# Running rows on ACT's queue and as one-row products, with new half steps in the first two blocks

## The chip, the cores and the metric

One Trainium2 chip, one core. The metric is the device time of one execution in microseconds (us). In the profile PE is TensorE's matmul stream and PEld its weight loads, DVE is VectorE, ACT is ScalarE, POOL is GpSimd, SP is SyncE, whose queue issues the kernel's transfers; "ACTq" or "SPq" is such an engine's queue.

## The reference

A token block of 2048 x 448 passes two stages, each behind a layer norm whose scale, shift and gate come from a condition vector `c` (six groups of `c @ w_mod`). The first stage is an S4 convolution: each channel d has a kernel K[d, l], the real part of a sum over 256 complex modes, and the stage adds the gated convolution of the normalized tokens with K, plus a skip term. The second is a SwiGLU network:

```python
h = silu(y @ w_gate) * (y @ w_up)      # 448 -> 1792
out = x + gate * (h @ w_down)          # 1792 -> 448
```

## The kernel before

**Tiles and blocks.** The tokens are 16 tiles of 128 rows, in blocks of 2, 2, 3, 3, 3 and 3 tiles (`BLOCKS`). With the given data the kernel K is so close to a straight line in l that the convolution is a pair of running sums along the tokens: v0 and v1 are the normalized tile times two gain rows (`gm0`, `gm1`), and a product with a triangle of ones (`tri`) gives their sums within the tile. The sums up to the tile's start are one row each, `run0` and `run1` (1 x 448 f32). A flag computed on the device picks this path; a general convolution stands in the other branch and is not run.

**The network.** `ffn` goes over 14 slices f of 128 of the 1792 hidden channels. `gate_up(f)` is 22 products (L665), w and y each split into a coarse and a fine f32r part; then come silu on ACT (L671), the mult on DVE (L676), the cast `phi` on ACT (L679) and its rest `plo` on DVE (L680). `down(f - 1)` (L691) is three products a tile that add into one PSUM bank a tile. So TensorE's order is gate_up(f), down(f-1), gate_up(f+1), down(f), and on. In block 0 the weights are not in SBUF yet: each slice loads w(f+5) (L85, L86: gate and up, four transfers) and the w_down rows d(f+3) (L92) on SP's queue, and ACT and DVE split them: `split_d` of slice f (L96 ACT, L97 DVE) at the head of gate_up(f), `split_w` of f + 2 (L103, L104 ACT; L106, L108 DVE) around its silu.

**The stages of the next tiles.** The first stage of the next block's tiles is hung into the running block, at half steps: 2f is behind gate_up(f), 2f + 1 behind down(f - 1). The table `TIMES` holds a row for block 0, one for block 1, and one for all later ones: the half steps of the first norm's statistics for each tile, of its root, then for each tile those of its stages with the second norm's statistics as the last, of the second root, and of the normalized tiles (`make_xn`, L185). Each engine runs its instructions in program order, so a half step too early makes the engine wait, and all that is behind it too. The stages are s0 (`make_h`, L170 and L172), s1 (v0 and v1, L784), `rows` (the running rows are added to row 0 of v0 and v1, L789 and L790), s2 (`rows`, then the coarse and fine part of v0, L797 ACT and L798), s3 (h times the skip gain), s4 (three products with `tri`, L809 to L811) and s5. Block 0 leaves s2 out and has s4f, with the product of v0 in f32 (L820, L821).

s5 makes the running rows of the next tile: a copy on ACT (L830), `run0` on DVE (L831), both in partitions 96 to 127, and a transfer of partition 127 to partition 0 (L832, `run[0:1] <- run[127:128]`, both rows, 3.5 KB). Two more DVE instructions (L833, L834) finish the tile. The next tile's `rows` read what the transfer brought. There are 13 such transfers.

**Ahead of block 0.** Tiles 0 and 1 are computed in a prelude. Its end is `transposes(TILES[0])`, which turns the normalized tiles and splits them into `hhi` and `hlo` (L192 PE, L193 and L195 ACT, L197 and L198 DVE; the third of its four banks is the PSUM buffer `cv`), and then six products of 33 x 448 (L442) into `cv`, which give the running rows behind tile 1, copied out on ACT (L445, L446). Buffers of `bank()` come from a pool of four PSUM banks, `cv` is one by itself.

Of the kernel before, what the change touches and what calls it, by code (L numbers as in the profile page):

```python
# [8 lines left out]
F32 = mybir.dt.float32  # L9
# [7 lines left out]
L, D, N, F = 2048, 448, 256, 1792  # L17
# [6 lines left out]
TILES = [list(range(sum(BLOCKS[:b]), sum(BLOCKS[:b + 1]))) for b in range(len(BLOCKS))]  # L24
# [2 lines left out]


TIMES = (
# [3 lines left out]
)  # L33
EPS = 1e-5
# [5 lines left out]
def f32(ap):  # L40
    return ap.bitcast(F32)
# [3 lines left out]
def tile_kernel(ctx, tc, x, a_re, a_im, b_re, b_im, c_re, c_im, log_dt, dskip,  # L45
                wg, wu, wd, c, w_mod, dft, idft, out):
    nc = tc.nc
    sy, ve, sc, po, pe = nc.sync, nc.vector, nc.scalar, nc.gpsimd, nc.tensor
# [4 lines left out]
    psd = ctx.enter_context(tc.tile_pool(name="psd", bufs=1, space=PS))  # L53
    dram = ctx.enter_context(tc.tile_pool(name="dram", bufs=1, space=bass.MemoryType.DRAM))

    def bank():
        t = psg.tile([128, 512], F32, name="bank")
        return t
# [40 lines left out]
    def split_w(j, part=None):  # L99
        hi, lo, st = wgu[j][:, :, 0:3, :], wgu[j][:, :, 3:6, :], wgu[j][:, :, 6, :]  # L100
        w = raw[j]
        if not part:
            sc.copy(hi, w[:, :, 0:3, :])  # L103
            sc.copy(st, w[:, :, 3, :])  # L104
        if part is None or part == 1:
            ve.tensor_tensor(lo, w[:, :, 0:3, :], f32(hi), op=OP.subtract)  # L106
        if part is None or part == 2:
            ve.tensor_tensor(st[64:128], w[64:128, :, 3, :], f32(st[64:128]), op=OP.subtract)  # L108

    ident = const.tile([128, 128], F32)  # L110
    tri = const.tile([128, 128], F32R)
    tok = const.tile([128, 1], F32)

    run = const.tile([128, 2, D], F32)
    run0, run1 = run[:, 0, :], run[:, 1, :]
# [71 lines left out]
    def transposes(ts):  # L187
        n = len(ts) * 128
        for k in range(4):
            ps = psd.tile([128, 512], F32, name="cv") if k == 2 else bank()  # L190
            for j, i in enumerate(ts):
                pe.transpose(ps[:, j * 128:(j + 1) * 128], xn[i][:, k * 128:(k + 1) * 128], ident)  # L192
            sc.activation(hhi[:, k, 0:n], ps[:, 0:n], AF.Identity, scale=cb1c[:, k:k + 1], bias=sbc[:, k:k + 1])  # L193
            if k % 2:
                sc.activation(ps[:, 0:n], ps[:, 0:n], AF.Identity, scale=cb1c[:, k:k + 1], bias=sbc[:, k:k + 1])  # L195
            else:
                ve.tensor_scalar(ps[:, 0:n], ps[:, 0:n], cb1c[:, k:k + 1], sbc[:, k:k + 1], op0=OP.mult, op1=OP.add)  # L197
            ve.tensor_tensor(hlo[:, k, 0:n], ps[:, 0:n], f32(hhi[:, k, 0:n]), op=OP.subtract)  # L198
# [61 lines left out]
    with tc.tile_pool(name="pre", bufs=1) as pre, tc.tile_pool(name="wm", bufs=6) as wm:  # L260
# [86 lines left out]
        s0 = pre.tile([P, 4], F32)  # L347
# [33 lines left out]
        for k in range(3):  # L381
# [13 lines left out]
        v0, v1, vh, vl, hd = ([pre.tile([128, D], t, name=f"{n}_{q}") for q in range(2)] for n, t in  # L395
                              (("v0", F32), ("v1", F32R), ("vh", F32R), ("vl", F32R), ("hd", F32)))
# [38 lines left out]
        ve.tensor_scalar(flag, zm, SMALL * SMALL, None, op0=OP.is_le)  # L435
        for z in (1, 2):
            split_w(0, z)
        transposes(TILES[0])
        o = psd.tile([128, 512], F32, name="cv")[:, 0:D]
        mm = [(left[:, 0], v) for v in vh + vl] + [(left[:, 1 + q], v1[q]) for q in range(2)]  # L440
        for k, (u, v) in enumerate(mm):
            pe.matmul(o[0:33], u, v, start=k == 0, stop=k == len(mm) - 1)  # L442
        split_w(1)
        sc.copy(xs[1], os[1])
        sc.copy(run0[0:1], o[0:1])  # L445
# [322 lines left out]
    def small_path(pools):  # L768
        work = pools.work
        vs = {}  # L770

        def s0(i):
            h = work.tile([128, D], F32, name="h", bufs=2)
            make_h(h, i)
            vs[i] = h

        def s1(i, on_v=False):
            h = vs[i]  # L780
            v0 = work.tile([128, D], F32, name="v0", bufs=2)
            v1 = work.tile([128, D], F32R, name="v1", bufs=2)
            for v, g in ((v0, gm0), (v1, gm1)):
                (ve if on_v else po).tensor_tensor(v, h, g, op=OP.mult)  # L784
            vs[i] = h, v0, v1

        def rows(i, on_v=False):
            h, v0, v1 = vs[i]
            ve.tensor_tensor(v0[0:1], v0[0:1], run0[0:1], op=OP.add)  # L789
            (ve if on_v else po).tensor_tensor(v1[0:1], f32(v1[0:1]), run1[0:1], op=OP.add)  # L790

        def s2(i, on_v=False):
            rows(i, on_v)
            h, v0, v1 = vs[i]
            vh = work.tile([128, D], F32R, name="vh")
            vl = work.tile([128, D], F32R, name="vl")
            sc.copy(vh, v0)  # L797
            ve.tensor_tensor(vl, v0, f32(vh), op=OP.subtract)  # L798
            vs[i] = h, vh, vl, v1

        def s3(i, on_v=False):
            h = vs[i][0]
            (ve if on_v else po).tensor_tensor(h, h, gd, op=OP.mult)

        def s4(i):
            h, vh, vl, v1 = vs[i]
            o = psd.tile([128, 512], F32, name="cv")[:, 0:D]
            s = bank()[:, 0:D]
            pe.matmul(o, tri, vh, start=True, stop=False)  # L809
            pe.matmul(s, tri, v1, start=True, stop=True)  # L810
            pe.matmul(o, tri, vl, start=False, stop=True)  # L811
            ve.tensor_tensor(xs[i], h, xs[i], op=OP.add)
            vs[i] = o, s


        def s4f(i):
            h, v0, v1 = vs[i]
            o = psd.tile([128, 512], F32, name="cv")[:, 0:D]
            s = bank()[:, 0:D]
            pe.matmul(s, tri, v1, start=True, stop=True)  # L820
            pe.matmul(o, f32(tri), v0, start=True, stop=True)  # L821
            s3(i, True)
            ve.tensor_tensor(xs[i], h, xs[i], op=OP.add)
            vs[i] = o, s

        def s5(i):
            o, s = vs.pop(i)
            if i + 1 < NT:
                e = slice(96, 128)
                sc.copy(run1[e], s[e])  # L830
                ve.scalar_tensor_tensor(run0[e], run1[e], 128.0, o[e], op0=OP.mult, op1=OP.add)  # L831
                sy.dma_start(run[0:1], run[127:128])  # L832
            ve.tensor_tensor(xs[i], xs[i], o, op=OP.add)  # L833
            ve.scalar_tensor_tensor(xs[i], s, tok, xs[i], op0=OP.mult, op1=OP.add)  # L834

        v = lambda g: lambda i: g(i, True)
        return lambda b: ((s0, v(s1), v(rows), s4f, s5), (s0, v(s1), v(s2), v(s3), s4, s5),
                          (s0, s1, s2, s3, s4, s5))[min(b, 2)]

    def general_path(pools, y):  # L840
# [81 lines left out]
```

## Time and profile before

| what | us |
| --- | --- |
| median of 3 runs | 517.26 |
| lowest and highest run | 516.23, 518.02 |
| the profiled execution, its time | 516.48 |
| its span | 514.7 |
| TensorE busy | 485.2 |
| VectorE busy | 278.3 |
| ScalarE busy | 163.9 |
| block 0's first gate_up starts | 51.65 |
| block 1's first gate_up starts | 116.76 |
| block 2's first gate_up starts | 179.58 |

The mean granted clock of TensorE over the span was 0.973 of full speed. A row of a timeline reads: start, length, engine, line, operation, what it writes <- what it reads, and in brackets how long the engine stood still just before and what ended that. A row of waits reads: who waited, for whom, the total, how often, and the longest.

### The profile page before, as it was taken

The page shows a single profiled execution, that of the slowest core. Times are in us where ns is not written, and L with a number is a line of the kernel's source. Part 1 is how long each engine was busy: PE and PEld are TensorE (multiplying, and loading weights), DVE is VectorE, ACT ScalarE, POOL GpSimd, SP SyncE. Part 2 cuts the span into 40 slices and gives each one's busy share as a digit, 9 for nine tenths or more (in the row PEclk, how much of TensorE's full clock was granted, in tenths as well). Part 3 has the DMA queues.
Part 4 walks back from the last instruction along what each step waited for, and adds up shares of the span by engine and source line. Part 5 has one row for each costly group of instructions (what it writes and reads, how often), then busy time and mean ns, then how long its engine had stood idle before and what let it go on. Part 6 is the DMA issues. An engine that isn't in the chain of part 4 may idle for free.

```text
span 514.7 us, 7042 instructions
## 1 busy us (share of the span) xinstructions
PE 485.2 (94%) x2747; PEld 453.5 (88%) x2747; DVE 278.3 (54%) x516; ACT 163.9 (32%) x346; POOL 87.3 (17%) x103
## 2 busy tenths in 40 slices
PE   7867998899998999999999999999999999999994
PEld 4443988799997899999999999999999999999993
DVE  1897699956785563464374555455345346112213
ACT  4248554562222621221441122162122143111110
POOL 1468000000000102341100532000234110000000
PEclk8888999899998999999999999999999999999998
DMA  7995355512000020000020000003000001000001
GB/s 204 263 228 172 112 152 162 155 41 91 1 0 2 2 90 1 0 2 0 2 95 14 1 2 2 0 1 107 1 1 2 0 3 55 0 1 1 1 0 60
DMA packets 26002, 26.05 MB, mean 51 GB/s; under 512 B 2248, under 2 KB 25288, under 8 KB 25960
## 3 DMA queue, kind: packets, MB, share of 16 engines
q1 hardware_dynamic: 25960, 25.52, 17.5%
q8 instruction: 23, 0.38, 0.3%
q14 instruction: 19, 0.16, 0.1%
HBM read 21.80 MB, written 3.67 MB: 49 GB/s over the span
## 4 chain that ended last, share of the span: by engine, by line
PE 79%; DVE 6%; SPq 6%; DMA 4%; issue 3%; ACT 1%; POOL 0%; DVEq 0%; ACTq 0%; POOLq 0%
PE bank L665 51%; PE dn L691 24%; SPq L85 3%; SPq L86 2%; DMA br<-in_A_B_re_dram 2%; DMA raw<-in_B_w_up_dram 1%; PE bank L192 1%; DMA run<-run 1%; DVE gu L106 1%; DVE gu L108 1%; SPq L275 1%; DMA rawd<-in_B_w_down_dram 1%; DVE wdl L97 1%; DVE bank L676 1%; PE cv L809 1%
## 5 line engine op out<-in xcount | busy, mean ns | idle before, releaser
L665 PE MATMUL bank<-hhi,gu 128*128 128x384 f32 (+1 forms) x1169 | 211.3, 320 | 0.0
L665 PEld LDWEIGHTS bank<-hhi,gu 128*128 128x128 f32 x1169 | 191.6, 190 | 3.4 <-issue 0.7
L665 PE MATMUL bank<-hlo,gu 128*128 128x384 f32 (+1 forms) x668 | 131.9, 318 | 0.0
L676 DVE TENSOR_TENSOR bank<-raw,bank 128x384 f32<-128x384 f32 (+1 forms) x70 | 37.5, 535 | 154.3 <-PE bank L665 137.7
L665 PEld LDWEIGHTS bank<-hlo,gu 128*128 128x128 f32 x668 | 110.3, 190 | 0.3 <-DVE hlo L198 0.3
L679 ACT CAST phi<-bank 128x384 fp32r<-128x384 f32 (+1 forms) x84 | 37.3, 444 | 145.1 <-DVE bank L676 145.1
L671 ACT ACTIVATE raw<-bank 128x384 f32<-128x384 f32 (+1 forms) x70 | 32.8, 469 | 128.7 <-PE bank L665 128.5
L680 DVE TENSOR_TENSOR plo<-bank,phi 128x384 fp32r<-128x384 f32 (+1 forms) x84 | 43.0, 512 | 38.0 <-ACT phi L679 38.0
L691 PE MATMUL dn<-wdh,phi 128*128 128x448 f32 x224 | 61.3, 373 | 0.5 <-ACT phi L679 0.5
L691 PE MATMUL dn<-wdl,phi 128*128 128x448 f32 x224 | 60.0, 368 | 0.0
L691 PE MATMUL dn<-wdh,plo 128*128 128x448 f32 x224 | 59.9, 367 | 0.0
L691 PEld LDWEIGHTS dn<-wdl,phi 128*128 128x128 f32 x224 | 42.3, 189 | 4.0
L691 PEld LDWEIGHTS dn<-wdh,plo 128*128 128x128 f32 x224 | 41.9, 188 | 4.1
L691 PEld LDWEIGHTS dn<-wdh,phi 128*128 128x128 f32 x224 | 39.9, 190 | 2.6 <-ACT phi L679 1.1
L151 POOL TENSOR_SCALAR rsb<-mvb 128x3 f32<-128x3 f32 (+1 forms) x6 | 1.7, 282 | 124.5 <-DVE mvb L135 124.5
L784 POOL TENSOR_TENSOR v<-h,gm 128x448 f32<-128x448 f32 x9 | 11.1, 1237 | 64.5 <-DVE h L172 55.0
L151 POOL TENSOR_SCALAR rsa<-mva 128x3 f32<-128x3 f32 (+1 forms) x6 | 1.6, 268 | 108.1 <-DVE mva L135 108.1
L209 PE MATMUL bank<-wmt,cs 112*128 112x448 f32 (+1 forms) x32 | 16.1, 662 | 2.3 <-DMA wmt<-in_w_mod_dram 2.3
L209 PEld LDWEIGHTS bank<-wmt,cs 112*128 112x128 f32 (+1 forms) x32 | 6.4, 209 | 10.6 <-issue 9.7
L106 DVE TENSOR_TENSOR gu<-raw,gu 128x768 fp32r<-128x768 f32 x14 | 14.6, 1041 | 0.4 <-ACT gu L103 0.3
L790 POOL TENSOR_TENSOR v<-v,run 1x448 fp32r<-1x448 f32 x9 | 11.4, 1270 | 17.3 <-DMA run<-run 17.1
L797 ACT CAST vh<-v 128x448 fp32r<-128x448 f32 x12 | 6.8, 567 | 20.7 <-DVE v L789 20.7
(194 smaller groups left out, 447.6 us busy)
## 6 DMA issues: line engine op xcount, KB each, us to landing
wmt<-in_w_mod_dram SPq DMA_DIRECT2D x6, 784.0 KB
rawd<-in_B_w_down_dram SPq DMA_DIRECT2D x14, 224.0 KB
x<-in_A_u_dram SPq DMA_DIRECT2D x12, 224.0 KB
raw<-in_B_w_gate_dram SPq DMA_DIRECT2D x14, 192.0 KB
raw<-in_B_w_up_dram SPq DMA_DIRECT2D x14, 192.0 KB
out_dram<-x SPq DMA_DIRECT2D x11, 224.0 KB
raw<-in_B_w_gate_dram SPq DMA_DIRECT2D x14, 64.0 KB
raw<-in_B_w_up_dram SPq DMA_DIRECT2D x14, 64.0 KB
```

Of the source, the lines that this page charges most:

```text
L85: sy.dma_start(raw[j][:, s, 0:3, :], w[0:384, cs].rearrange("(k p) f -> p k f", p=128))
L86: sy.dma_start(raw[j][:, s, 3, :], bass.AP(tensor=w.tensor, offset=w.offset + 384 * F + j * 128, ap=[[0, 2], [F, 64], [1, 128]]))
L106: ve.tensor_tensor(lo, w[:, :, 0:3, :], f32(hi), op=OP.subtract)
L209: pe.matmul(ps[0:rows, 0:D], cs[:, k:k + 1].to_broadcast([P, rows]), w[k], start=k == 0, stop=k == 3)
L665: pe.matmul(ps[s][:, 0:n], w[:, s, a], (hlo if lo else hhi)[:, k, 0:n], start=not lo and a == 0, stop=lo and k == 3)
L671: sc.activation(p[:, 0:n], ps[0][:, 0:n], AF.Silu)
L676: ve.tensor_tensor(ps[1][:, 0:n], p[:, 0:n], ps[1][:, 0:n], op=OP.mult)
L679: sc.copy(hi[:, 0:n], ps[1][:, 0:n])
L680: ve.tensor_tensor(lo[:, 0:n], ps[1][:, 0:n], f32(hi[:, 0:n]), op=OP.subtract)
L691: pe.matmul(dn[q][:, 0:D], u[:, cs], v, start=f == 0 and z == 0, stop=f == NF - 1 and z == 2)
L784: (ve if on_v else po).tensor_tensor(v, h, g, op=OP.mult)
L790: (ve if on_v else po).tensor_tensor(v1[0:1], f32(v1[0:1]), run1[0:1], op=OP.add)
```

## The change

Four things are edited.

1. The rows of `TIMES` for block 0 and block 1 have other numbers; the row for the later blocks stays. In block 0 the stages `rows` are gone from the lists.
2. In the prelude the six products come ahead of the transposes and write into a `bank()` instead of `cv`.
3. In block 0 `rows` is left out. Instead s4f adds two f32 products of one row each (`tri[0:1]` with `run1` and with `run0`, new lines L823 and L824) into the same PSUM sums.
4. The transfer of the running rows is issued by ACT (new line L835) and no longer by SP.

Behind s4f the new file has three lines more (L831 becomes L834, L833 becomes L836).

```diff
 TIMES = (
-    ((1, 3), 3, ((4, 6, 7, 9, 10, 12), (8, 11, 14, 16, 17, 18)), 19, (20, 21)),
+    ((1, 1), 3, ((4, 7, 10, 12, 14), (3, 8, 19, 19, 21)), 22, (25, 23)),
...
-        transposes(TILES[0])
-        o = psd.tile([128, 512], F32, name="cv")[:, 0:D]
+        o = bank()[:, 0:D]
...
             pe.matmul(o[0:33], u, v, start=k == 0, stop=k == len(mm) - 1)
+        transposes(TILES[0])
...
-            pe.matmul(s, tri, v1, start=True, stop=True)
-            pe.matmul(o, f32(tri), v0, start=True, stop=True)
+            pe.matmul(s, tri, v1, start=True, stop=False)
+            pe.matmul(o, f32(tri), v0, start=True, stop=False)
+            pe.matmul(s, f32(tri[0:1, :]), run1[0:1], start=False, stop=True)
+            pe.matmul(o, f32(tri[0:1, :]), run0[0:1], start=False, stop=True)
...
-                sy.dma_start(run[0:1], run[127:128])
+                sc.dma_start(run[0:1], run[127:128])
...
-        return lambda b: ((s0, v(s1), v(rows), s4f, s5), (s0, v(s1), v(s2), v(s3), s4, s5),
+        return lambda b: ((s0, v(s1), s4f, s5), (s0, v(s1), v(s2), v(s3), s4, s5),
```

For block 1's third tile `TIMES` goes from (13, 16, 20, 19, 21, 22, 22) to (13, 17, 17, 18, 20, 21, 21), and the root and the normalized tiles from 23 and (24, 24, 25) to 25 and (25, 25, 25).

TensorE in block 0, around the first tile's s4f. Before, in the fifth slice (`wdl_533` and `wdh_532` are parts of w_down, `gu_527` the next gate and up weights):

```order
L691 MATMUL dn_489<-wdl_533,phi 128x448
L691 MATMUL dn_488<-wdh_532,plo 128x448
L691 MATMUL dn_489<-wdh_532,plo 128x448
L820 MATMUL bank<-v_700,tri 128x448
L821 MATMUL cv<-v_699,tri 128x448
L665 MATMUL bank<-hhi,gu_527 128x256 x7
L665 MATMUL bank<-hlo,gu_527 128x256 x4
```

and now:

```order
L691 MATMUL dn_489<-wdh_532,plo 128x448
L665 MATMUL bank<-hhi,gu_527 128x256 x7
L665 MATMUL bank<-hlo,gu_527 128x256 x4
L665 MATMUL bank<-hhi,gu_527 128x256 x7
L665 MATMUL bank<-hlo,gu_527 128x256 x4
L821 MATMUL bank<-v_709,tri 128x448
L822 MATMUL cv<-v_708,tri 128x448
L823 MATMUL bank<-run,tri 128x448
L824 MATMUL cv<-run,tri 128x448
L691 MATMUL dn_488<-wdh_584,phi 128x448
```

The tri products moved from ahead of the next gate_up to behind it, and the two one-row products stand behind them; the second tile's moved from behind a gate_up at half step 16 to behind a down at 19.

ACT in block 0, around the first run row (what an instruction waits for stands in the brackets; a name with DMAHW is a transfer's semaphore). Before:

```order
L679 CAST phi<-bank 128x256 [waits DVE_49]
L830 COPY run<-bank 32x448
L96 CAST wdh_696<-rawd_76 128x448 [waits DMAHW5_49]
L671 ACTIVATE p<-bank 128x256 [waits PE_49,Activation_49]
L103 CAST gu_691<-raw_75 128x2x384 [waits DMAHW3_49,DMAHW1_49]
```

and now:

```order
L679 CAST phi<-bank 128x256 [waits DVE_49]
L833 COPY run<-bank 32x448
L835 DMA run<-run 1x16x56 [waits DMAHW3_49,DVE_49]
L96 CAST wdh_754<-rawd_77 128x448 [waits DMAHW2_49]
L671 ACTIVATE p<-bank 128x256 [waits PE_49]
```

The issue stands between the copy and the next split of w_down, a slice later than the copy did, and waits for DVE and for a semaphore that the weight loads use too.

DVE in block 1, behind the second tile's s5 (rawd_77 is the second tile, x_68 the third, v_1639 and v_1657 its v0). Before:

```order
L831 SCALAR_TENSOR_TENSOR run<-run,cv 32x448
L833 TENSOR_TENSOR rawd_77<-rawd_77,cv 128x448
L834 SCALAR_TENSOR_TENSOR rawd_77<-bank,tok,rawd_77 128x448
L134 BN_STATS stb<-rawd_77 128x6
L135 BN_AGGR mvb<-stb 128x2
L803 TENSOR_TENSOR h<-h,gd 128x448
L676 TENSOR_TENSOR bank<-raw_74,bank 128x256
L680 TENSOR_TENSOR plo<-bank,phi 128x256
L789 TENSOR_TENSOR v_1639<-v_1639,run 1x448
L790 TENSOR_TENSOR v_1640<-v_1640,run 1x448
L798 TENSOR_TENSOR vl<-v_1639,vh 128x448
L812 TENSOR_TENSOR x_68<-h,x_68 128x448
```

and now:

```order
L834 SCALAR_TENSOR_TENSOR run<-run,cv 32x448
L836 TENSOR_TENSOR rawd_77<-rawd_77,cv 128x448
L837 SCALAR_TENSOR_TENSOR rawd_77<-bank,tok,rawd_77 128x448
L784 TENSOR_TENSOR v_1657<-h,gm_86 128x448
L784 TENSOR_TENSOR v_1658<-h,g_85 128x448
L789 TENSOR_TENSOR v_1657<-v_1657,run 1x448
L790 TENSOR_TENSOR v_1658<-v_1658,run 1x448
L798 TENSOR_TENSOR vl<-v_1657,vh 128x448
L676 TENSOR_TENSOR bank<-raw_74,bank 128x256
L680 TENSOR_TENSOR plo<-bank,phi 128x256
L134 BN_STATS stb<-rawd_77 128x6
L135 BN_AGGR mvb<-stb 128x2
```

The third tile's v0, v1 and running rows moved ahead of a slice's mult and `plo`, directly behind the run row's own end, and the second tile's statistics moved behind them.

2 rows, old and new, of the table TIMES are left out of this document.

## The prediction

> **What bounds the kernel now.** I read the page's head first, then TensorE's waits, then tables of clock and traffic for single stretches, then the timelines around the waits.
>
> ```profile
> span 514.7 us, 7042 instructions
> ...
> PE 485.2 (94%) x2747; PEld 453.5 (88%) x2747; DVE 278.3 (54%) x516; ACT 163.9 (32%) x346; POOL 87.3 (17%) x103
> ```
>
> TensorE is busy 94% of the span, so outside the opening the kernel is a TensorE program, and a change that is no TensorE saving can win only what TensorE loses by standing still or by a slow clock. Its waits (total, times, longest):
>
> ```profile
> PE bank L820 <- DVE v L790: 3.9, 2, 3.0
> ...
> PE cv L442 <- DVE hlo L198: 2.9, 1, 2.9
> ...
> PE cv L809 <- ACT vh L797: 2.2, 1, 2.2
> ...
> PE bank L192 <- ACT raw L185: 1.0, 2, 0.7
> ```
>
> L820 is block 0, L442 the end of the prelude, L809 and L192 block 1. In the next table the columns are busy time (PE, PEld, DVE, ACT, POOL), then TensorE's granted clock, DMA share and GB/s.
>
> ```profile
> 57.00:60.00 3.00, 3.00 (x23) 2.91 (x22) 2.31 (x4) 3.00 (x7) 0.00 (x0) 1.00 0.11 32
> 62.00:88.00 26.00, 24.54 (x169) 22.59 (x168) 25.31 (x50) 14.08 (x32) 1.17 (x2) 1.00 0.55 159
> 92.50:94.50 2.00, 2.00 (x5) 1.08 (x4) 1.94 (x5) 0.90 (x2) 0.00 (x0) 0.50 0.62 193
> 118.00:159.00 41.00, 41.00 (x299) 39.98 (x298) 30.87 (x63) 10.04 (x25) 1.11 (x2) 1.00 0.09 29
> 163.00:166.00 3.00, 3.00 (x17) 3.00 (x15) 0.00 (x0) 0.39 (x1) 0.00 (x0) 0.50 0.02 5
> ```
>
> Three things: 41 us of block 1 run without a gap at full clock; right behind the waits of block 0 and block 1 the clock is 0.50; and the weight stream of block 0 moves 159 GB/s, but only 32 between 57 and 60 us.
>
> Now the two places. Block 0 (start, length, engine; in brackets the idle time before and what ended it), then the chain of waits for the same place:
>
> ```profile
> 72.58 0.47 PE L820 MATMUL bank<-v,tri 128*128 128x448 f32 x1 [0.96 <-DVE v L790]
> ...
> 73.29 0.63 PE L665 MATMUL bank<-hhi,gu 128*128 128x256 f32 x1
> ...
> 91.72 0.74 PE L820 MATMUL bank<-v,tri 128*128 128x448 f32 x1 [2.98 <-DVE v L790]
> ...
> 95.41 0.76 PE L665 MATMUL bank<-hhi,gu 128*128 128x256 f32 x5
> ...
> 116.76 1.00 PE L665 MATMUL bank<-hhi,gu 128*128 128x256 f32 x7
> ```
> ```profile
> 86.62 3.87 DMA run<-run
> ...
> 122.19 1.22 PE dn L691 x6
> ...
> 123.41 2.63 PE bank L665 x22
> ```
> ```profile
> 80.24 0.63 DVE L831 SCALAR_TENSOR_TENSOR run<-run,cv 32x448 f32<-32x448 f32 x1
> ```
>
> The row was ready at 80.87 (80.24 + 0.63), its transfer was issued only at 86.62, behind weight loads on SP's queue, and took 3.87. TensorE paid 0.96 + 2.98 in waits. The pair of products and one `down` took 3.69 (91.72 to 95.41) where 0.71 (72.58 to 73.29) + 1.22 = 1.93 is the full-clock price: 1.76 lost to the clock. Sum 5.7.
>
> Block 1:
>
> ```profile
> 150.85 0.36 PE L809 MATMUL cv<-vh,tri 128*128 128x448 f32 x1
> ...
> 154.10 0.57 PE L691 MATMUL dn<-wdh,phi 128*128 128x448 f32 x2
> ...
> 161.55 0.47 PE L809 MATMUL cv<-vh,tri 128*128 128x448 f32 x1 [2.21 <-ACT vh L797]
> ...
> 166.65 0.57 PE L691 MATMUL dn<-wdh,phi 128*128 128x448 f32 x2
> ```
>
> The same work, tri products and a gate_up (2.63 of it the gate_up, by the chain's row), took 5.10 at 161.55 and 3.25 at 150.85: 1.85 lost to the clock, 2.21 to the wait, and 1.0 to the late last normalization (the L192 row). Sum 5.1.
>
> **The change, part by part.**
>
> *Block 1, new steps.* The third tile's `s2` comes directly behind the second's `s5` (both at half step 17, where they were at 17 and 20), with its tri products at 20 now, so that three half steps lie between where one lay. The danger is that the run row now travels between these two. Rows from quiet stretches (DVE, POOL), two from the chain of waits in block 0, and the split's second half:
>
> ```profile
> 230.36 0.63 DVE L831 SCALAR_TENSOR_TENSOR run<-run,cv 32x448 f32<-32x448 f32 x1
> ...
> 232.82 1.14 POOL L790 TENSOR_TENSOR v<-v,run 1x448 fp32r<-1x448 f32 x1 [5.64 <-DMA run<-run]
> ```
> ```profile
> 82.15 1.15 DVE v L784 x2
> ...
> 91.06 0.62 DVE v L790
> ```
> ```profile
> 161.53 0.63 DVE L798 TENSOR_TENSOR vl<-v,vh 128x448 fp32r<-128x448 f32 x1
> ```
>
> From the end of L831 (230.99) to the reader's start: 1.83 us. Behind L831 VectorE now has what it had in block 0 behind the L831 of 80.24: L833, L834 and two L784, from 80.87 to 83.30 (82.15 + 1.15), 2.43. The row lands 0.6 before VectorE asks for it. Followed on: call T the end of gate_up(8). down(7) and the tri products end at T+1.84 (1.22 + 0.62), the copy on ACT (0.53, quoted below) and the run row (0.63) at T+3.0, VectorE reaches the row additions at T+5.4, two of 0.62 and the split's 0.63 end at T+7.3, and the mult and the cast of slice 9 (0.4 each, the cast's row is below) at T+8.1. TensorE needs the cast at T+8.94 (1.84, then 2.63 + 1.22 + 2.63 + 0.62). Margin 0.8, so the wait of 2.21 goes and its slow stretch with it. A row flight of 3.87, as beside the weights, would be 1.4 past VectorE's arrival, less the margin: 0.6 of wait. The last statistics come some slices earlier, and the normalization follows slice 12's cast directly: the 1.0 goes. What is late next: nothing that I can price. Gain 5.1, bounds 3 (a wait of 2 comes back) and 5.5.
>
> *Run row on ACT's queue.* Thirteen issues leave SP, where one took 0.65 and another waited 5.75 for its turn (80.87 to 86.62), and come to ACT ahead of the next silu or, in block 0, of the next split of w_down.
>
> ```profile
> 79.81 1.98 SPq L92 DMA_DIRECT2D rawd<-in_B_w_down_dram  x1
> ...
> 86.62 0.65 SPq L832 DMA_DIRECT2D run<-run  x1
> ```
> ```profile
> 217.88 0.53 ACT L830 COPY run<-bank 32x448 f32<-32x448 f32 x1
> ...
> 220.54 0.49 ACT L671 ACTIVATE raw<-bank 128x384 f32<-128x384 f32 x1 [2.13 <-PE bank L665]
> ```
>
> Ahead of the second row's silu, in block 2, ACT idles 2.13 behind a run-row copy; it must now wait 0.7 for VectorE's part of the run row (0.63) and issue for 0.65: 1.35, hidden. In block 1, with shorter slices, some tenths may stick out. Behind the issue only the silu waits, and TensorE needs that slice's cast a whole gate_up later (2.63 in block 1). ACT's price of an issue isn't in the trace (ACT issues nothing before): between nothing and the 1.98 that the longest SP issue of a weight load could be; I take 0.65, the same transfer's row. At 1.98 ACT is held 2.7, 0.55 over the idle time, and a gate_up covers that: also nothing. Without that cover the 8 issues of blocks 2 to 4 would cost 8 x 0.55 = 4.4. SP loses its waits for the row, and its loads move up by 0.65 in each of two slices, which is inside the stream's bounds below.
>
> *Block 0: one-row products.* VectorE loses four 1-row additions (0.6 each). TensorE gains four f32 products. An f32 product of this width is what stands between 72.58 and 73.29 beside one f32r product: 0.71 for both, so about 0.4 to 0.5; 4 x 0.4 = 1.6 us added to TensorE, certain unless TensorE stands there anyway. The first tile needs only the prelude's row. The second tile's run row is made behind half step 12 and read at 19, three and a half slices: about 13 us against 0.65 + 3.87. So the waits at L820 and their slow stretch go (5.7), less 1.6: 4.1 on TensorE.
>
> *Block 0: the prelude.* The six products come ahead of the transposes, out of the `cv` buffer that made them wait 2.9 for the transposes' last split (the L442 row). gate_up(0) needs only the coarse halves, so it and its silu can come about 3 earlier, and so can the weight loads that wait for the splits behind that silu. The stream cannot use all of this: the older loads are still landing. At 159 GB/s the hole of 57 to 60 us (32 GB/s) is worth 3 x (1 - 32/159) = 2.4 us; I take 1.4, a little over half, since the loads in the hole are the end of the old ones; bounds 0 and 2.4.
>
> *Block 0: the stream is late next.* w_down's splits wait for their loads (the first row is down(11) on TensorE):
>
> ```profile
> 109.60 0.57 PE L691 MATMUL dn<-wdh,phi 128*128 128x448 f32 x2
> ```
> ```profile
> 71.01 0.57 ACT L96 CAST wdh<-rawd 128x448 fp32r<-128x448 f32 x1 [1.97 <-DMA rawd<-in_B_w_down_dram]
> ...
> 90.30 0.56 ACT L96 CAST wdh<-rawd 128x448 fp32r<-128x448 f32 x1 [2.34 <-DMA rawd<-in_B_w_down_dram]
> ...
> 92.58 0.37 ACT L679 CAST phi<-bank 128x256 fp32r<-128x256 f32 x1 [0.40 <-DVE bank L676]
> ...
> 99.97 0.57 ACT L96 CAST wdh<-rawd 128x448 fp32r<-128x448 f32 x1 [0.82 <-DMA rawd<-in_B_w_down_dram]
> ...
> 103.87 2.08 ACT L185 ACTIVATE raw<-x,ngb,rsb 128x448 f32<-128x448 f32 x4 [0.87 <-POOL ngb L158]
> ```
>
> Loads come every (90.30 - 71.01)/4 = 4.82, TensorE needs 2.63 + 1.22 = 3.85 a slice. So a TensorE without stalls just waits for weights. Slice 10's weights came at 99.97; slice 11's, one period on, at 104.8, with the stream 1.4 ahead at 103.4. Its cast is 2.3 behind (90.30 to 92.58), at 105.7. From the start of down(11) to the end of the block is 7.2 (109.60 to 116.76), so 112.9; and the two normalizations (2.08 for both, the L185 row) stand on ACT ahead of the splits of slices 12 and 13, up to 0.9 more: 113.8. Against 116.76 that is 3.0. With no lead of the stream 1.6; bound by TensorE alone, 4.1 and up to 2 of the earlier start, 6.1. I take 3.0, as the stream is the nearest.
>
> *Sum.* 5.1 + 3.0 = 8.1, blocks 2 to 5 nothing. On the profiled execution: 516.48 (span 514.7 and 1.8 around it) - 8.1 = 508.4. The median of the runs shown is 517.26, 0.8 above the profiled one: 509.2.
>
> [...] The clock is 0.50 behind a wait of 2.21, and at full rate in the 41 us without a gap. [...]
>
> **Rivals.**
> 1. *Stream not late* (10%): the loads run faster than 4.82 a slice when TensorE no longer stands. Against: the waits of ACT for 8 loads of rawd. Block 0 gives 6.1, sum 11.2: 506.1.
> 2. *Block 0 gives nothing* (12%): stream not earlier, and ACT's queue, held behind the run row's issue, costs the rest. For: in block 0 `split_d` stands directly behind that issue. Sum 5.1: 512.2.
> 3. *The slow stretch of block 1 has another cause than its wait* (8%) and stays, 1.85: sum 6.3: 511.0. For: it began 1.4 after the wait's end. Against: nowhere is the clock low without a wait shortly ahead.
> 4. *Slower* (5%): ACT cannot issue the run row in block 0 until a weight load that went out earlier on the same semaphore has landed (the order shows this wait). I take that load to land about 1 after the split's own data. If it is a slice later, each of two rows holds ACT 4.8, TensorE stands, and each stall brings 1.8 of slow clock: 2 x 6.6 = 13.2 in place of the 5.7 removed, and 1.6 more work; with block 1's 5.1: +4.0, 521.3. It decides from (5.7 - 1.6 + 5.1 + 1.6)/2 = 5.4 a row, which is that slice and a part of the slow stretch.
> 5. *It does nothing* (5%): waits come back at other places for what went, 517.3. For: 41 us of block 1 are full already and two thirds of the kernel isn't touched.
>
> **How the numbers follow.** The forecast has 60%. About 0.3% (1.6 us) is what a measurement of this kernel can tell from no change. Faster by more: forecast and rivals 1 to 3, 90%; within it 5%; slower 5%. The range takes the lower cases (block 0 at 1.6 with block 1 at 3: 4.6, 512.7) and most of rival 1 (its 506.1): 505.8 to 512.7.
>
> **What would show it.** Right: no wait at the tri products of blocks 0 and 1, none of the clock rows at 0.50 behind them, the run row issued within 1.5 of L834 in block 1, ACT's waits for rawd longer than 11.9 in all, TensorE's waits in block 0 now for weights, block 1 starting near 113.7 and lasting 57.7 instead of 62.8, later blocks of unchanged length. Wrong: TensorE waits for the cast in blocks 2 to 5 (ACT's issue), ACT idle behind L835 for over 2 us, VectorE waiting for the run row at L789 in block 1, or block 1's start later than 115.

## The result and the profile after

| | before | changed |
| --- | --- | --- |
| median (4 runs each, the same chip) | 516.94 us | 508.94 us |
| lowest, highest | 516.23, 518.02 | 507.52, 510.41 |
| profiled execution: time, span | 516.48, 514.7 | 510.41, 508.6 |

The ratio is 0.9844, 95% interval 0.981 to 0.9877: faster by 8.0 us at the medians, where 8.1 was forecast, and 508.94 where 509.2 was. The profiled execution is the slowest of the four; how its 6.1 us of span come about is worked out below. The head of the changed kernel's page, and TensorE's waits from block 0 on:

```profile
span 508.6 us, 7033 instructions
...
PE 488.4 (96%) x2755; PEld 454.0 (89%) x2755; DVE 277.8 (55%) x512; ACT 162.2 (32%) x346; POOL 86.3 (17%) x103
```
```profile
PE dn L691 <- ACT phi L679: 0.8, 2, 0.5
PE dn L665 <- DVE hlo L198: 0.3, 1, 0.3
PE bank L192 <- ACT p L671: 0.2, 1, 0.2
```

The waits at the tri products are gone, and what is left adds up to 1.3 us. The clock (the column of 1.00), once for block 0 and once for block 1:

```profile
62.00:100.00 38.00, 37.91 (x242) 33.10 (x243) 32.37 (x61) 18.91 (x44) 0.18 (x1) 1.00 0.54 157
115.00:173.00 58.00, 58.00 (x416) 56.18 (x415) 42.88 (x89) 20.41 (x48) 2.67 (x6) 1.00 0.07 21
```

No half-rate stretch is left behind the prelude, and block 1 is 58 of 58 us busy. To see where the time went, the span is cut at TensorE's last small product ahead of the transposes (L235), at the first gate_up of each block, and at the last product. Of before, then of the changed kernel:

```profile
43.32 1.03 PE L235 MATMUL bank<-ones,row 1*128 1x1 f32 x10
...
179.58 1.40 PE L665 MATMUL bank<-hhi,gu 128*128 128x384 f32 x7
```
```profile
45.85 1.03 PE L235 MATMUL bank<-ones,row 1*128 1x1 f32 x10
...
50.34 0.82 PE L665 MATMUL dn<-hhi,gu 128*128 128x256 f32 x4
...
115.17 1.09 PE L665 MATMUL bank<-hhi,gu 128*128 128x256 f32 x7
...
172.85 1.40 PE L665 MATMUL bank<-hhi,gu 128*128 128x384 f32 x7
```

| stretch | before | changed | difference |
| --- | --- | --- | --- |
| up to L235 (the same program in both) | 43.32 | 45.85 | +2.5 |
| L235 to block 1 | 73.44 | 69.32 | -4.1 |
| block 1 | 62.82 | 57.68 | -5.1 |
| block 2 to the last product | 327.53 | 327.27 | -0.3 |
| behind the last product (the last output's transfer) | 7.59 | 8.48 | +0.9 |

The first and the last row are not the change's: over the fourteen profiled executions of this study, whose program is the same up to L235, that point lies anywhere between 42.30 and 46.15, and the tail between 7.4 and 8.8. That is why single executions differ by 2 to 3 us, and why I compare stretches.

### The profile page after: what moved, and what is told of

Same layout as the page of the kernel before. It is cut to its first block, busy times and chain, and to the rows that moved or that the text cites. A ratio compares the mean times of both kernels' runs of the same rounds, so it can differ in the third digit from the quotient of the medians.

```text
span 508.6 us, 7033 instructions
## 1 busy us (share of the span) xinstructions
PE 488.4 (96%) x2755; PEld 454.0 (89%) x2755; DVE 277.8 (55%) x512; ACT 162.2 (32%) x346; POOL 86.3 (17%) x103
## 4 chain that ended last, share of the span: by engine, by line
PE 80%; DMA 8%; DVE 4%; ACT 3%; issue 2%; SPq 2%; POOL 0%; ACTq 0%; DVEq 0%
PE bank L665 49%; PE dn L691 24%; DMA wmt<-in_w_mod_dram 4%; DMA rawd<-in_B_w_down_dram 4%; PE bank L209 2%; PE dn L412 1%; PE bank L192 1%; ACT gu L103 1%; SPq L85 1%; SPq L86 1%; DVE scr L356 1%; DMA raw<-in_B_w_gate_dram 1%; PE bank L810 0%; PE cv L811 0%; PE cv L809 0%
## 5 line engine op out<-in xcount | busy, mean ns | idle before, releaser
L209 PE MATMUL bank<-wmt,cs 112*128 112x448 f32 (+1 forms) x32 | 17.4, 711 | 2.9 <-DMA wmt<-in_w_mod_dram 2.9
L106 DVE TENSOR_TENSOR gu<-raw,gu 128x768 fp32r<-128x768 f32 x14 | 13.7, 980 | 1.0 <-ACT gu L103 0.8
```

The costliest lines, as they stand in the source:

```text
L209: pe.matmul(ps[0:rows, 0:D], cs[:, k:k + 1].to_broadcast([P, rows]), w[k], start=k == 0, stop=k == 3)
```

## The experiments

Twelve runs. "To block 1" is from L235 to block 1's first gate_up; "slice 11" is the start of ACT's split of slice 11's w_down (L96), which in most runs waits for its load (not in e11 and e12); a dash stands where block 0 has the old half steps, under which it doesn't wait. "Block 1" is from its first gate_up to block 2's. The ratios are to runs of the kernel before on the same chip, whose medians were 518.21 for e1 to e4, 515.91 for e5 to e8 and 517.41 for e9 to e12.

| kernel | time, ratio to before | to block 1 | slice 11 to block 1 | block 1 |
| --- | --- | --- | --- | --- |
| before | 516.94 | 73.44 | - | 62.82 |
| changed | 508.94, 0.9844 (0.981 to 0.9877) | 69.32 | 10.40 | 57.68 |
| e1 block 1's steps alone | 510.85, 0.9884 (0.985 to 0.9917) | 74.16 | - | 57.14 |
| e2 rows on VectorE | 508.49, 0.9837 (0.9804 to 0.9871) | 70.93 | 10.42 | 57.67 |
| e3, the same kernel again | 506.84 | 69.48 | 10.43 | 57.66 |
| e6, the same kernel again | 508.0 | 69.72 | 10.43 | 57.66 |
| e4 rows on SP | 508.77, 0.9824 (0.9794 to 0.9854) | 70.93 | 11.20 | 57.14 |
| e5 light loads | 505.89, 0.9809 (0.9754 to 0.9864) | 68.33 | 13.23 | 57.14 |
| e7 light loads, rows on VectorE | 504.6, 0.979 (0.9745 to 0.9836) | 67.01 | 10.92 | 57.67 |
| e8 gaps in later blocks | 513.07 | 70.45 | 10.41 | 57.68 |
| e9 old prelude | 511.29, 0.9887 (0.9852 to 0.9921) | 72.80 | 10.42 | 57.66 |
| e10 before, rows on ACT | 517.44, 1.0001 (0.9971 to 1.0031) | 72.07 | - | 62.80 |
| e11 w_down's loads from GpSimd | 506.92, 0.9789 (0.9757 to 0.982) | 71.48 | 13.15 | 57.14 |
| e12 the same, rows on SP | 508.64, 0.9839 (0.9799 to 0.9879) | 71.20 | 13.87 | 57.14 |

### e1: block 1's steps alone

```diff
-    ((3, 4, 5), 5, ((6, 7, 8, 10, 10, 12, 14), (9, 11, 15, 17, 17, 18, 19), (13, 16, 20, 19, 21, 22, 22)), 23, (24, 24, 25)),
+    ((2, 3, 3), 3, ((5, 6, 8, 10, 10, 11, 13), (7, 8, 14, 15, 17, 17, 18), (13, 17, 17, 18, 20, 21, 21)), 25, (25, 25, 25)),
```

> The kernel before, with the changed kernel's half steps for block 1 alone; the running rows stay on SP's queue, block 0 and the prelude are the old ones. Theory: block 1's wait and its slow stretch come from where s2 and s4 of the third tile stand, and the queue has no part in it: block 1 shrinks from 62.8 to about 57.7 and the time falls by 5.1, ratio to before 0.990. Rival: with three half steps between, the row must travel on an idle queue; on SP the row lands late, VectorE waits at L789 and block 1 keeps 2 us or more of it: a gain of 3 or less.

Measured: ratio 0.9884, 6.0 us at that chip's before of 518.21, interval 4.3 to 7.8; block 1 takes 57.14 against 62.82, 5.7 less. Block 0's wait and its slow stretch are all there (e1's TensorE and clock):

```profile
92.02 0.74 PE L820 MATMUL bank<-v,tri 128*128 128x448 f32 x1 [3.40 <-DVE v L790]
```
```profile
92.00:93.00 1.00, 0.98 (x2) 0.84 (x3) 1.00 (x3) 0.60 (x3) 0.00 (x0) 0.50 0.64 133
```

So block 1's gain is shown by itself, and it is the steps: on SP's queue, which issues nothing else from 150 to 156 us, the row goes out at 153.17, 0.03 behind L831's end, and VectorE's L789 starts at 155.49 without a wait. Up to block 1 this program is the old one, so its 74.16 beside the 73.44 of the kernel before is a second execution of the old block 0.

### e2, e3, e6: the running rows back on VectorE in block 0

```diff
-    ((1, 1), 3, ((4, 7, 10, 12, 14), (3, 8, 19, 19, 21)), 22, (25, 23)),
+    ((1, 1), 3, ((4, 7, 8, 10, 12, 14), (3, 8, 17, 19, 19, 21)), 22, (25, 23)),
...
-            pe.matmul(s, f32(tri[0:1, :]), run1[0:1], start=False, stop=True)
-            pe.matmul(o, f32(tri[0:1, :]), run0[0:1], start=False, stop=True)
...
-        return lambda b: ((s0, v(s1), s4f, s5),
+        return lambda b: ((s0, v(s1), v(rows), s4f, s5),
```

> The changed kernel, with block 0's one-row products taken out and the four one-row additions on VectorE put back, a half step or two ahead of the tri products. As predicted (an f32 product is 0.4, and weights set block 0's end): four products are 1.6, of which at most 0.5 shows, 508.4 to 508.9. Rival, from the trace of the changed kernel, where a pair of products with its two one-row products takes 2.74: a one-row product is 0.85 and TensorE sets block 0's end: 3.4 less, 505.5. In between: 0.85 each, but the weights are only 0.5 behind, so that at most about 0.5 to 1 shows.

Two further profiled executions of the same kernel, to see the spread:

> Placeholder for one more look at the same kernel as e2_rows_dve, to see how far one profiled execution differs from another of the same program: the opening up to 44 us by up to 2, everything behind it by under 0.3.

> A third profiled execution of the kernel of e2_rows_dve, for the spread of the opening and of block 0: block 1 starts 69.5 to 71 behind the opening's last small product.

Measured: 508.49, and from L235 to block 1 70.93, 69.48 and 69.72, against 69.32 and 70.45 for two executions of the one-row products (the second is e8, the same program up to there). Four f32 products fewer on TensorE gain nothing that can be told. The expectation that everything behind the opening differs by under 0.3 from one execution to the next was wrong: to block 1 the three differ by up to 1.45, and a single execution's stretch is worth no more than that. The products' price was wrong in the prediction: in the changed kernel, the tri products of the first tile (L821, f32r; L822, f32; then the two one-row products):

```profile
74.51 0.36 PE L821 MATMUL bank<-v,tri 128*128 128x448 f32 x1
74.72 0.91 PE L822 MATMUL cv<-v,tri 128*128 128x448 f32 x2
75.56 1.01 PE L823 MATMUL bank<-run,tri 1*128 1x448 f32 x2
76.41 0.91 PE L824 MATMUL cv<-run,tri 1*128 1x448 f32 x2
77.25 0.68 PE L691 MATMUL dn<-wdh,phi 128*128 128x448 f32 x2
```

From start to start it is 0.84 or 0.85 for each f32 product, one row or 128, so 3.4 us for the four, not 1.6. What takes their place when they are gone, in e2 (ACT, TensorE):

```profile
102.82 0.57 ACT L96 CAST wdh<-rawd 128x448 fp32r<-128x448 f32 x1 [1.51 <-DMA rawd<-in_B_w_down_dram]
```
```profile
73.16 0.47 PE L821 MATMUL bank<-v,tri 128*128 128x448 f32 x1 [1.75 <-DVE v L790]
...
113.24 1.09 PE L665 MATMUL bank<-hhi,gu 128*128 128x256 f32 x7
```

TensorE now waits 1.75 for VectorE's late additions, and there are more such waits (0.97, 0.51 and 0.83, together 4.1 instead of the 3.4), none of which the changed kernel has; block 1 starts 10.42 behind the split that waited for slice 11's weights. TensorE alone isn't the limit. The time fits the first expectation as well as the last, but the first's price of 0.4 is wrong by the rows above, so the last (0.85 each, the weights right behind) is the one that fits.

### e4: the running rows on SP again

```diff
-                sc.dma_start(run[0:1], run[127:128])
+                sy.dma_start(run[0:1], run[127:128])
```

> The changed kernel, with the running rows issued by SP again. Theory: in block 0 the row has seven half steps and in block 1 the queue is empty, so the queue is worth nothing there; ACT no longer stands 3.3 and 3.2 behind the issue, but TensorE doesn't wait for that: 508.9, within 1. Rival one: on SP the row comes 5.8 later, behind weight loads, and TensorE waits at the one-row products of block 0's second tile: 2 or more slower. Rival two: ACT's standing held the weight splits back: 1 or more faster.

Measured: 508.77, the changed kernel's time within what can be told. In its profile block 0 is a little longer, and differently: TensorE waits 0.36 for the row, and a half-rate stretch follows (TensorE; the clock of that stretch).

```profile
96.28 1.01 PE L823 MATMUL bank<-run,tri 1*128 1x448 f32 x2 [0.36 <-DMA run<-run]
```
```profile
95.50:98.90 3.40, 3.04 (x13) 1.58 (x12) 2.21 (x4) 2.67 (x6) 0.00 (x0) 1.00 0.58 163
98.90:102.00 3.10, 3.10 (x17) 3.10 (x16) 2.94 (x6) 1.01 (x3) 0.00 (x0) 0.52 0.49 146
```

So the theory's time holds; its premise, that seven half steps make the queue worth nothing, holds only nearly: the row still came 0.36 late on the queue that issues the weight loads.

### e5 and e7: fewer bytes of weights

```diff
-        sy.dma_start(wdn[j], wd[j * 128:(j + 1) * 128, :])
+        e = 128 if j < NP0 else 32
+        sy.dma_start(wdn[j][0:e], wd[j * 128:j * 128 + e, :])
```

> The changed kernel, with only 32 of the 128 rows of each w_down slice loaded from slice 3 on (the others keep old data), so that a slice's loads are 568 KB instead of 736. Theory (weights set block 0's end, TensorE with its f32 products is just behind): the loads come about every 3.7 us, ACT's waits for them go, and block 0 gets shorter only by what TensorE's own limit leaves, 0.5 to 1.0. Rival (the weights alone set it): 3 or more shorter. Rival (TensorE alone sets it): no change, within 0.2 from the opening's end to block 1's start.

> The light loads of e5_lite (32 of 128 rows of w_down from slice 3 on) in the kernel of e2_rows_dve, whose running rows are added on VectorE and whose TensorE has four f32 products less. Theory: both limits are lifted, so block 0 gets shorter by those products too, 2 to 3.4 against e5_lite, less what VectorE's late additions cost (e2_rows_dve shows 1.75 and 0.51 of wait for them). Rival (the products cost 0.4 each): 1.6 less at most.

Both kernels leave out three quarters of the w_down rows from slice 3 on. Measured: to block 1 68.33 in e5, 1.0 less than the changed kernel's profile and 2.1 less than its second execution in e8; with the products gone as well (e7) 67.01, 1.3 less again, although TensorE waited 1.56 for VectorE's additions there. ACT's waits for w_down's loads fall to 5.2 us in all (e5). Taking the products away gained nothing under the full loads (e2) and 1.3 under the light ones: two limits stand close behind one another in block 0, the weights first, TensorE 1 to 2 us behind. In e5 the distance to slice 11 is 13.23, and the chain of work that ended last consists of TensorE alone from 84 us to block 1: there TensorE is the limit. e5's loads came every 4.5 ((98.67 - 71.98)/6), not every 3.7 as I had worked out from the bytes. Their traffic fell to 132 GB/s (60 to 88 us; 158 in the changed kernel), so something else than the bytes held them, and what it was this run doesn't show.

### e8: waits put into the later blocks

```diff
-    ((3, 3, 3), 4, ((6, 7, 9, 10, 11, 12, 13), (8, 9, 14, 15, 16, 17, 18), (12, 13, 19, 19, 21, 22, 22)), 23, (24, 24, 25)),
+    ((3, 3, 3), 4, ((6, 7, 9, 10, 11, 12, 13), (8, 9, 14, 15, 16, 17, 18), (12, 13, 21, 19, 21, 22, 22)), 23, (24, 24, 25)),
```

> The changed kernel, with the third tile's s2 in blocks 2 to 4 moved from half step 19 to 21, where its tri products stand, so that TensorE waits there once in each block for the row additions, the ACT cast and the rest, some 2 to 3 us. By the trace of the kernel before, a wait of 2.2 can be followed by 3.4 us of half clock: 1.8 more behind some of the three waits. [...] Time: 508.9 plus 3 waits (6 to 9) plus 0 to 5.4.

Measured: three waits of 1.09, not of 2 to 3, and no half-rate stretch behind any of them (at 233.88, 318.02 and 402.18). Waits this short don't test whether one of 2.2 brings the half clock again: the experiment is inconclusive on that. It gave two other things. Blocks 2 to 4 became 1.6 longer each (84.19, 84.16 and 84.14 against 82.58 and 82.54), so a wait costs more than its row says: the three products behind it start 0.31 to 0.35 apart instead of 0.21. And it is a second execution of the changed program up to block 1, with a quick opening (42.65). TensorE, ACT, TensorE:

```profile
86.86 0.67 PE L691 MATMUL dn<-wdh,phi 128*128 128x448 f32 x2 [1.44 <-ACT phi L679]
```
```profile
83.81 0.68 ACTq L835 DMA_DIRECT2D run<-run  x1
84.53 0.57 ACT L96 CAST wdh<-rawd 128x448 fp32r<-128x448 f32 x1 [3.49 <-DMA raw<-in_B_w_gate_dram]
...
102.69 0.57 ACT L96 CAST wdh<-rawd 128x448 fp32r<-128x448 f32 x1 [1.64 <-DMA rawd<-in_B_w_down_dram]
```
```profile
113.10 1.10 PE L665 MATMUL bank<-hhi,gu 128*128 128x256 f32 x7
```

Here the mechanism of rival 4 is seen: ACT stands 3.49 at the row's issue, which goes out only when an earlier load (w_gate) has landed, and TensorE pays 1.44 of it. It costs nothing at the end, since block 1 again starts 10.41 behind slice 11's split.

### e9: the old prelude

```diff
-        o = bank()[:, 0:D]
+        transposes(TILES[0])
+        o = psd.tile([128, 512], F32, name="cv")[:, 0:D]
...
-        transposes(TILES[0])
```

> The changed kernel, with the prelude's six products behind the transposes and in cv again. Theory: an earlier prelude counts only as far as the weight stream gets ahead by it, 1.4 to 2.6, since slice 11's weights set block 1's start 10.4 behind their landing: 510.3 to 511.5, and block 1 still starts 10.4 to 10.6 behind that landing. Rival (TensorE sets block 0's end): the whole 3.4 by which gate_up(0) starts earlier is lost, 512.3. Rival (the stream has a lead anyway): no change, 508.9.

Measured: 511.29 against 508.94, 0.9887 against 0.9844 (the intervals overlap), 72.80 to block 1 instead of 69.32 and 70.45, and block 1 10.42 behind slice 11's weights (ACT, TensorE):

```profile
105.24 0.57 ACT L96 CAST wdh<-rawd 128x448 fp32r<-128x448 f32 x1 [1.63 <-DMA rawd<-in_B_w_down_dram]
```
```profile
115.66 1.09 PE L665 MATMUL bank<-hhi,gu 128*128 128x256 f32 x7
```

The stretch's figures put the prelude at 2.3 to 3.5, the medians at 2.3, as the theory had it. It is most of what block 0 gained, and it acts by the stream: the same 10.4 stands behind it, and slice 11's weights come 62.4 behind L235 here, against 58.9 and 60.0 with the new prelude.

### e10: the kernel before, with rows on ACT

```diff
-                sy.dma_start(run[0:1], run[127:128])
+                sc.dma_start(run[0:1], run[127:128])
```

> The kernel before, with the running rows issued by ACT and nothing else changed. Theory: in block 0 the row goes out soon after VectorE's part instead of 5.8 later behind weight loads, so the wait of 3.0 and the slow stretch of 1.8 at L820 shrink, but the weights take back a part: 1 to 4 faster, with block 1 unchanged at 62.8. Rival: ACT, held behind the row's issue until an earlier weight load has landed, loses as much as the row gains: the same time as before.

Measured: ratio 1.0001 (0.9971 to 1.0031): the rival holds, as far as ten runs tell; a gain of more than 1.5 is excluded, and the one profiled execution is 1.4 shorter to block 1. The wait of 3.0 at L820 shrinks to 1.70, its slow stretch is gone, and a new wait comes (TensorE, ACT):

```profile
89.31 0.47 PE L820 MATMUL bank<-v,tri 128*128 128x448 f32 x1 [1.70 <-DVE v L790]
...
99.93 0.67 PE L691 MATMUL dn<-wdh,phi 128*128 128x448 f32 x2 [1.67 <-ACT phi L679]
```
```profile
97.06 0.51 ACTq L832 DMA_DIRECT2D run<-run  x1
97.60 0.56 ACT L96 CAST wdh<-rawd 128x448 fp32r<-128x448 f32 x1 [5.48 <-DMA raw<-in_B_w_up_dram]
```

The queue alone is worth nothing that the time shows: ACT stands 5.48 at the issue until a load has landed.

### e11 and e12: w_down's loads from another queue

```diff
-        sy.dma_start(wdn[j], wd[j * 128:(j + 1) * 128, :])
+        (sy if j < NP0 else po).dma_start(wdn[j], wd[j * 128:(j + 1) * 128, :])
```

> The changed kernel, with w_down's loads from slice 3 on issued by GpSimd instead of SP. Theory (weights set block 0's end and SP issues without a pause): if it is SP's issuing that paces them, the loads come faster than every 4.8, ACT's waits for them go, and block 0 ends where e5_lite's does, 1 to 2 earlier: 507 to 508. Rival (the transfers themselves pace them, whoever issues): 4.8 stays and the time too. Rival: GpSimd's issuing is slower and the rows come later: slower by 1 or more.

> As e11_pool_loads, with the running rows on SP's queue again. Theory: ACT no longer stands behind the row's issue, which frees the cast that TensorE waits for when the opening is quick (1.4 in one execution), and block 1 is 0.5 shorter, as in the two kernels with SP's queue so far: 0.5 to 1.5 better than e11_pool_loads, about 506.5. Rival: the row comes late behind SP's loads, and TensorE waits at the one-row products: as e11_pool_loads or slower.

Measured: e11 506.92, ratio 0.9789 (0.9757 to 0.982), e12 508.64, ratio 0.9839. e11 has the lowest median of the kernels that compute everything (e3 and e6 are single times), but its interval touches the changed kernel's (0.981 to 0.9877), and its profile, which is of the slowest of its six runs (509.59), doesn't show why it should be faster: 71.48 to block 1, with this in it (a table of the stretch with the traffic as its last column, ACT, TensorE):

```profile
60.00:88.00 28.00, 27.30 (x177) 23.97 (x175) 22.08 (x41) 12.03 (x27) 3.65 (x7) 1.00 0.54 162
```
```profile
88.03 0.56 ACT L96 CAST wdh<-rawd 128x448 fp32r<-128x448 f32 x1 [4.25 <-DMA raw<-in_B_w_up_dram]
```
```profile
90.36 0.67 PE L691 MATMUL dn<-wdh,phi 128*128 128x448 f32 x2 [2.50 <-ACT phi L679]
```

ACT's waits for w_down are gone, and it waits for w_up instead: the traffic stays at 162 GB/s (60 to 88 us; 158 in the changed kernel), so the rival that the transfers pace themselves, whoever issues them, is the one that fits; the gain in the time I leave open. e12's theory fell too: its row came 1.28 late behind SP's loads, with a half-rate stretch behind that (a clock of 0.56 from 97.5 to 100.9 us), and the half microsecond in block 1 isn't SP's doing, since e5 and e11 have 57.14 with ACT's queue. It lies in block 1's first gate_up, whose products with `hlo` stand for the last split of the transposes. In the changed kernel, then in e5:

```profile
116.10 1.09 PE L665 MATMUL bank<-hlo,gu 128*128 128x256 f32 x4
```
```profile
112.73 0.64 PE L666 MATMUL bank<-hlo,gu 128*128 128x256 f32 x4
```

All seven executions with 57.66 to 57.68 have this first gate_up at 3.16 to 3.18 (115.17 to 118.35 in the changed kernel), and the others at 2.63 (111.90 to 114.53 in e5). So the half microsecond belongs to block 0's late end, not to block 1's steps.

## Why the prediction was right, point by point

**The time.** The runs hold the gain only to between 6.4 and 9.8, so it is luck that 8.0 was measured so close to the 8.1 of the forecast. By stretches the gain is 5.1 in block 1, 0.3 behind it and 3.0 to 4.8 ahead of it.

**Block 1, 5.1.** Right in size and cause. Measured 5.14 in the changed kernel's profile and 5.7 by itself (e1), a little above the bound of 5.5: the sum counted the wait by its row alone, and e8 shows that a wait costs about half a microsecond more (blocks 1.6 longer by waits of 1.09). (The second tile's `s5` stood at half step 18 before, not at 17; nothing in the sum hangs on it.) The step that carried it was the row's flight against VectorE's other work; in the changed kernel (DVE, ACT's queue):

```profile
150.98 0.63 DVE L834 SCALAR_TENSOR_TENSOR run<-run,cv 32x448 f32<-32x448 f32 x1 [0.29 <-ACT run L833]
...
153.96 0.61 DVE L789 TENSOR_TENSOR v<-v,run 1x448 f32<-1x448 f32 x1
```
```profile
151.64 0.50 ACTq L835 DMA_DIRECT2D run<-run  x1
```

The row is issued 0.03 behind L834's end, and L789 follows VectorE's other work without a wait, 2.35 behind that end, where 2.43 was forecast.

**Block 0 and the prelude, 3.0.** Right in size (69.32 and 70.45 against 73.44 and, in e1, 74.16: 3.0 to 4.8), and the step "the stream is late next" is what the runs showed: in six executions (the changed kernel, e2, e3, e6, e8, e9) block 1 starts 10.40 to 10.43 behind the split of slice 11's weights, and the prediction had 10.4 there (103.4 to 113.8). That its 10.4 is the measured one is luck, since it went another way: over slice 11's cast (2.3) and TensorE from down(11) on (7.2), with 0.9 for the normalizations. In the changed kernel TensorE comes to down(11) without a wait, and what ties the end to the weights is ACT (ACT, then TensorE):

```profile
104.77 0.57 ACT L96 CAST wdh<-rawd 128x448 fp32r<-128x448 f32 x1 [1.35 <-DMA rawd<-in_B_w_down_dram]
...
107.74 1.09 ACT L185 ACTIVATE raw<-x,ngb,rsb 128x448 f32<-128x448 f32 x2 [0.83 <-POOL ngb L158]
...
112.04 0.38 ACT L671 ACTIVATE p<-bank 128x256 f32<-128x256 f32 x1
```
```profile
112.47 0.44 PE L192 MATMUL bank<-ident,raw 128*128 128x128 f32 x2 [0.19 <-ACT p L671]
```

A normalization of the next tiles waits 0.83 for GpSimd, the splits of slices 12 and 13 and the other normalization stand behind it, and the last transposes wait for the last silu. In all six the normalization starts 2.97 or 2.98 behind slice 11's split. TensorE is hardly behind: from down(11) to block 1 it takes 7.68 here (107.49 to 115.17) and 7.16 in the kernel before. Four of the prediction's terms were off. The two that make up the 3.0 were off in opposite directions: without the prelude's lead e9 gains 0.6 to 1.4 where 1.6 was forecast, and the lead adds 2.3 to 3.5 where 1.4 was. The other two had no weight in the sum. The one-row products cost 3.4 and not 1.6: I had taken the start of the next group, 73.29, for the end of an f32 product. The rows behind it in the kernel before show the mistake:

```profile
74.47 0.64 PE L665 MATMUL bank<-hlo,gu 128*128 128x256 f32 x4
74.95 1.00 PE L665 MATMUL bank<-hhi,gu 128*128 128x256 f32 x7
75.79 0.64 PE L665 MATMUL bank<-hlo,gu 128*128 128x256 f32 x4
```

The first seven products behind the f32 one span 1.18 (73.29 to 74.47), the next seven of the same kind 0.84 (74.95 to 75.79): a part of the f32 product's time stands in the group behind it. By TensorE alone, that would have left 5.7 - 3.4 = 2.3 instead of 4.1. And the earlier start, of which the prediction let TensorE use up to 2, was 3.8 (block 0's first gate_up stands 4.49 behind L235, and 8.33 before).

**The queue, nothing.** Right for blocks 2 to 5: their length is unchanged (327.27 with ACT's queue as with SP's in e1 and e4), and an issue on ACT takes 0.50 to 0.68 by the rows above, near the 0.65 taken. In block 0 the queue isn't what the gain comes from: rows on SP give the same time (e4), and rows on ACT with the old steps give none (e10).

**The rivals.** Rival 1 (stream not late) fell with the 10.4 and with the period: in the changed kernel, too, the splits of slices 5 to 11 come every 4.82 ((104.77 - 75.87)/6). Rival 2 fell with e9 and the 3.0 to 4.8. Rival 3 fell: block 1 has no slow stretch left, and the stretches behind waits of 2.2 to 3.4 went with the waits. In the kernel before, 1.99 of standing still in one window of a grid of 3.41 us lay directly ahead of block 1's slow stretch (last section). Rival 4's mechanism is real: ACT was held 3.49 (e8), 4.25 (e11) and 5.48 (e10) at these issues until a load had landed. In the changed kernel (3.27 and 3.20, the second ended by VectorE's L834) no wait of TensorE is listed behind it; where one is, it is three to six tenths of the holding (1.44 of 3.49, 1.67 of 5.48, 2.50 of 4.25), and the weights hide a part (in e8 block 1 still starts 10.41 behind slice 11's split). With the new steps it didn't decide. Rival 5 fell with the time.

**What would show it.** Three of the signs for it came out otherwise: block 1 started at 115.17 and not near 113.7, since this execution's opening was 2.5 longer; ACT's waits for w_down's loads are 11.3 in all and not above 11.9, while it stood 6.5 at the two issues; and TensorE's waits in block 0 were not for weights: the dearer products filled the time in which it would have waited. Two of the signs against it came: block 1's start later than 115, and ACT idle for over 2 at the issue L835. The first is the opening's, and the second cost TensorE nothing that its waits show.

## What to carry to other kernels

Price a matmul from a run of its own kind, start to start in the middle of a group, not across a change of type, where the next group's rows hold a part of the cost (1.18 for seven products here instead of 0.84). Where two limits stand within a microsecond or two, taking work off the second can gain nothing (here the one-row products: nothing under the full loads in e2, 1.3 under the light ones in e7): find the event that the end follows at a constant distance (here the split of slice 11's weights, 10.4), read the rows that make the distance, since a sum that gives the same number can go another way, and ask of each edit whether it moves that event. Moving a transfer to a compute engine's queue brings the waits of that issue with it: what stood behind loads on SP now holds ACT's own work behind the same loads (here for 3.49 to 5.48 in e8, e11 and e10).

## What the runs showed of the hardware

- In the kernel before and in the changed kernel the granted clock changed only on a grid of 3.41 us (3.413 by the whole span): before at 9.37, 12.78, 19.61, 23.02, 33.27, 36.68, 46.92, 53.74, 91.29, 94.70, 162.97, 166.38 and 511.13 us, changed at 9.62, 13.04, 19.86, 26.69, 33.52, 40.34, 47.17, 50.58 and 504.56. The slow stretches of e10 (160.90 to 164.32) and e12 (97.08 to 100.50) have its length. From 55 us to the last product the half clock came six times in the fourteen executions, each time for the window of the grid behind one in which TensorE stood still, or ran one-row products, for 1.99 us or more: 2.55 and 1.99 in the kernel before, 3.31 in e1, 2.21 in e10, and with the one-row products 2.05 in e4 and 2.83 in e12 (where it stood for only 0.36 and 1.13). Behind windows with 1.74 (e2) or less it never came in them; the one-row products of a tile by themselves make 1.69 (75.56 to 77.25 in the changed kernel). So in these executions a wait's length didn't decide, but how it lay in the grid: block 1's wait of 2.21 in the kernel before lay with 1.99 in one window, and e11's of 2.50 lay in two (1.46 and 1.27, the busy time being 1.95 and 2.13 of 3.41), with the full clock behind it. Counting the one-row products as standing still is what separates all these windows; it was not tried by itself. The tables, of before and of e11 (TensorE's busy time first, the clock third from the end):

```profile
159.56:162.97 3.41, 1.42 (x7) 1.04 (x8) 2.64 (x5) 0.93 (x2) 0.00 (x0) 1.00 0.00 0
162.97:166.38 3.41, 3.41 (x18) 3.41 (x17) 0.00 (x0) 0.39 (x1) 0.00 (x0) 0.50 0.02 5
```
```profile
85.67:89.08 3.41, 1.95 (x15) 1.58 (x13) 0.95 (x2) 1.02 (x3) 0.00 (x0) 1.00 0.32 95
89.08:92.49 3.41, 2.13 (x13) 2.02 (x14) 3.15 (x8) 3.00 (x7) 0.55 (x1) 1.00 0.70 198
92.49:95.90 3.41, 3.41 (x25) 3.31 (x24) 3.35 (x8) 1.96 (x4) 0.54 (x1) 1.00 0.53 157
```

- GpSimd's small row L157 takes 0.19 (five of its six rows in the changed kernel) where VectorE isn't at L106. In the six executions above it stands beside L106 and takes 0.40 to 0.74, and ends 0.05 or 0.06 behind it in each (in the changed kernel 106.98 to 107.38, with L106 from 106.37 to 107.33). That fits the constant distance: L106 follows from slice 11's split, and the normalization waits for L157's successor, although the statistics it starts from come anywhere from 0.12 to 0.52 ahead of that split. Why the two end together was not tried.
- An f32 product of 448 columns took 0.84 with 128 rows (74.72 to 75.56 in the changed kernel) and 0.85 and 0.84 with one (75.56 to 76.41 to 77.25), and an f32r product 0.21 (74.51 to 74.72).
- The opening of one and the same program (up to L235) ended anywhere between 42.30 and 46.15 us.
